# Some scaled copies of V on GpSimd, the gate in four pieces, new lengths and half sets in a planned attention kernel

## The chip, the cores and the metric

The kernel runs on one core of one Trainium2 chip. The metric is the time of the program on the device in microseconds (us), taken as the median of its runs. A core has five engines with one instruction queue each: TensorE (PE, matrix products), VectorE (DVE), ScalarE (ACT, here mostly exponentials), GpSimd (POOL) and SyncE (SP, which starts transfers). Each engine works through its own queue in order; semaphores tie the queues together.

## The reference

The input `x` has 2048 rows of 512 elements. Two blocks work on it and a gate mixes them:

```python
qkv = (x @ wqkv)...                      # 32 heads of 16
# block A
p = softmax(einsum("bhqd,bhkd->bhqk", q, k) * 16 ** -0.5)
a = einsum("bhqk,bhkd->bhqd", p, v) @ woA
# block B: linear attention, phi(t) = where(t > 0, t + 1, exp(t)) + 1e-6
num = phi(q) @ (phi(k)^T v);  den = phi(q) . sum(phi(k));  b = (num / den) @ woB
g = sigmoid((x * gate_w).sum(-1, keepdims=True))
return g * a + (1 - g) * b
```

Block A is nearly all of the work: 32 heads x 2048 x 2048 exponentials.

## The kernel before

**Rounds and units.** Block A runs in 32 rounds. A round is 4 heads against 512 queries; it is cut into 64 units, each of 128 keys of one head by 512 queries, so there are 2048 units in all. A unit takes one score product on PE ("QK": `ps<-Qpad,KT`, 512 columns), an exponential, and a product with V on PE.

**Two ways to the exponential.** Most units go to ACT (line 2063): one ACTIVATE takes the scores of two or three units out of PSUM, 1024 or 1536 columns wide, and writes `PT`. Other units are "claimed" for DVE (line 1565): DVE writes an integer into `DP` whose bits, read as a float, approximate the exponential. Such a unit is needed in three copies with shifted integers. Four claimed units make one tile of `DP`; the two shifted copies of a tile are made by one addition each, on POOL (line 1609) or on DVE (line 1606). Each of the three copies is multiplied by V times a weight of its own, so V is kept with the weights 1, 203/256 and 161/256. The two scaled copies of V exist only for the last six of the 16 key blocks (`KB2 = 10`), and claims come only from there. They are made in `step_V` (lines 895 to 927), by DVE (line 925): 288 or 576 columns each, 16 instructions in the whole kernel.

**Sets.** PE multiplies four units at once, one in each quarter of its columns: four matmuls of 32 output rows and 512 columns, called a set here (`pv_cols`, from line 1339). A set with `DP` is `ps<-DP,Vaug`, one with `PT` is `ps<-PT,Vaug`. In the last round, after 44 of the 64 units, the products are done the other way round, as matmuls of 52 columns (`ps<-Vaug,DP`, `ps<-Vaug,PT`).

**The ring.** The scores of a group of units (one ACTIVATE) lie in one of two slots of three PSUM banks (banks 0 to 2 and 3 to 5). PE may write the scores of group g+2 when ACT has read group g. Between two groups of score products PE does other work, called a gap here: sets, pieces of the projections, of block B and of the output, and fills (products with a tile of zeros, `ps<-warm`, which keep PE active).

**The planner.** The order of every queue is written out by a planner that runs when the kernel is built. It keeps a clock for each engine, adds a fixed length for each piece (`SET_T` for a set, `MM512` for a matmul of 512 columns, `QK_T` for the scores, `SWITCH_T` for a change of PE's tiling), and in the loop at lines 2089 to 2107 fills the gap after each group: sets when more than `PV_LAG` products wait, then a piece of another step (`misc_step`), then sets again, then fills. How many sets go into a gap is `room`: the time left before the next scores are late for ACT (`t_late`, with a reserve of `MARGIN`), divided by `SET_T`, plus `ROOM`, rounded down, at most `MOST`. Further constants bound claims (`CLAIM_LOAD`, `STARVE`), the lending of score banks (`LEND`), and the fills (`FILL_AHEAD`).

**DVE and POOL.** DVE's work waits in `items` and is picked by `pump`; an item with a second form may go to POOL (`pool_go`), unless DVE has work of its own that should go first (`YIELD`, `YIELD_SOON`).

**The gate.** `step_gate` (from line 937) multiplies `x` by `gate_w`: 64 matmuls of one column, in 16 pieces of four (`GATE_N = 1`), each piece in a gap of its own or beside sets.

**The end.** After the last exponential PE finishes the products of the last round, DVE normalises it (lines 1322, 1323), PE transposes it, adds the last block's output product, and four tiles of 128 rows are scaled and stored by ACT and DVE (lines 2159 and 2165).

Of the kernel before, what the change touches and what calls it, by code (L numbers as in the profile page):

```python
# [17 lines left out]
STATS = {}  # L18
# [165 lines left out]


LAT = 0.11
SET_T = 0.218
MM512 = 0.216
QK_T = 0.324

PVW = 26
WIDE_MAC = 0.4
PV_T = 0.1012
PV_MAC = 0.087
SWITCH_T = 0.095
SELF_T = 0.08
ROWS_SEEN = 0.0
ACT_END = 0.25
# [14 lines left out]
def bass_gated_mix__mha_block__linear_attn_block__prompt_kernel(  # L213
# [33 lines left out]
    with ExitStack() as es:  # L247
# [192 lines left out]
        port_ev = [None]  # L440
        boost = [None]
        ADD_W = 0.4
        YIELD = 1.2
        YIELD_SOON = 0.5
        POOL_TT = 1.3
        POOL_V = 0.9
        POOL_ADD = 1.97
        OT_POOL = 1
        V2_POOL = 0

        def conflicts(op_, reads, writes):
            r2, w2 = op_[1], op_[2]
# [231 lines left out]
        def f_mm(o, l, r, start=True, stop=True, sg=False):  # L684
            return lambda: nc.tensor.matmul(o, lhsT=l, rhs=r, start=start, stop=stop, skip_group_check=sg)  # L685
# [5 lines left out]
        def f_tr(o, i):  # L691
# [12 lines left out]
           dur=1.6)  # L704
# [225 lines left out]

        gate_done = []

        GATE_N = 1
        GATE_AT = 3.5
        GATE_MAC = 0.45

        def step_gate(**kw):
            rd = xt_all + [r_gw]
# [397 lines left out]
        done_j = {}  # L1336
        PV_UNITS = 2

        def pv_cols(now, r, force, want, most, least):

            urgent = sum(1 for e in pv_pending if e[3] in r_PT) > PT_URGENT
            mine = [e for e in pv_pending if e[0] == r]
            by_j = [collections.deque() for _ in range(4)]

            def ready(e):
                return not e[3].pw and e[3].tw + LAT <= now + 0.03 and v_ready(r, e[1])

# [10 lines left out]
            while len(sets) < most:  # L1358
# [12 lines left out]
            fns, rds = [], []  # L1371
            for s in sets:
                STATS["sets"] = STATS.get("sets", 0) + 1
                STATS["in_sets"] = STATS.get("in_sets", 0) + len(s)
                for e in s:
                    if not v_ready(r, e[1]):
                        ensure(lambda: v_ready(r, e[1]))
                    half = rounds[r][2]
                    kb, j = e[1] // 4, e[1] % 4
                    (p_ap, z), = e[2]  # L1380
                    v0 = v_of(t8 % 2, kb, 2 * j + half, z)
                    w = bass.AP(tensor=v0.tensor, offset=v0.offset, ap=[list(v0.ap[0]), [1, 32]])
                    fns.append(f_mm(acc[32 * j:32 * j + 32, :], w, p_ap, start=j not in started, stop=False, sg=True))
# [5 lines left out]
                    acc_n[0] += e[4]  # L1389
                    done_j[(r, j)] = done_j.get((r, j), 0) + e[4]  # L1390
                    pv_pending.remove(e)
            pe_macro(fns, reads=rds, writes=[r_acc], dur=SET_T * len(sets), mac=0.2 * len(sets), mode="cols")
            fresh[0] = False
            if acc_n[0] == NU:
                assert r < NR - 1
                round_end(r)
                acc_round[0] += 1
                acc_n[0] = 0
                fresh[0] = True
            elif r == NR - 1 and acc_n[0] >= PART:  # L1400
                assert len(started) == 4
                part[0] = 1
                fresh[0] = True
                push(0, [(lambda: nc.vector.tensor_copy(epool[:, 0, :], acc), [r_acc], [r_e[0]], d_psum(512), None),
                         (lambda: nc.vector.tensor_tensor(epool[:, 1, :], acc, epool[:, 0, :], ALU.subtract), [r_acc, r_e[0]], [r_e[1]],
                          d_psum(512), None)])
            return True
# [18 lines left out]
        def pv_step(now, force=False, want=None, most=3, least=4):  # L1426

            r = acc_round[0]
            if r >= NR:
# [12 lines left out]
            if fresh[0]:  # L1442
                started.clear()
            if r < NR - 1 or part[0] == 0:
                return pv_cols(now, r, force, want, most, least)
            if add_part(False):
                return True
            most = PV_UNITS * most
            sel = []
            if want is not None:  # L1450
# [401 lines left out]
        A_FIRST = 200  # L1852
        LATE_END = 0
# [126 lines left out]
        while True:  # L1980
# [112 lines left out]
            while PE.t < t_lim - 0.05:  # L2093
                pump(PE.t)
                behind = sum(1 for e in pv_pending if e[3] in r_PT) > (PV_LAG if act_round[0] < NR - 1 else LAG_END)
                enter = SWITCH_T if pe_mode[0] == "full" else 0.0
                room = min(MOST, int((t_late - PE.t - enter) / SET_T + ROOM))
                if behind and room > 0 and pv_step(PE.t, most=room, least=3):
                    continue
                if g > last_stage and misc_step(PE.t, t_late):  # L2100
                    continue
                if not behind and room > 0 and pv_step(PE.t, most=room):
                    continue
                if PE.t + FILL_T < t_lim and mac_until(max(t_lim, PE.t + FILL_AHEAD)) < (MAC_END if acc_n[0] >= END_FROM else MAC_LOW) and fill(PE.t):
                    continue
                PE.t += 0.05
# [248 lines left out]
```

## Time and profile before

| | |
|---|---|
| runs | 675.3, 675.98, 675.98 us, median 675.98 |
| the profiled execution | 675.2 us, of which the span from first to last instruction is 673.4 us |
| TensorE clock granted | 1.000 |
| ACT busy | 660.0 us (98%), 715 instructions |
| PE busy | 655.0 us (97%) |
| DVE busy | 576.0 us (86%) |
| POOL busy | 550.8 us (82%) |

"Busy" is the union of the instructions' records on an engine, and a matmul's record includes its way through the array, so records overlap. In the tables of groups a row gives the line, the engine, the operation, output and input with their shapes, the count, then busy time and mean duration in ns, then the idle time just before, with what ended it. In the timeline a row gives the start, the length, and a number of merged instructions.

### The profile page before, as it was taken

What the parts mean: (1) busy time and instruction counts of PE and PEld (TensorE: products, weight loads), DVE (VectorE), ACT (ScalarE), POOL (GpSimd) and SP (SyncE); (2) the same over time, 40 slices, a digit from 0 to 9 for tenths busy, and PEclk for the clock granted to TensorE, in tenths of its full rate; (3) what the DMA queues carried; (4) which work ended last, traced back from release to release, by engine and by line L of the source; (5) the groups of instructions that cost most, each with busy time, mean ns of one, the idle gap of its engine ahead of it and who ended that gap; (6) DMA issues with size and microseconds to landing.
All of it is one profiled execution on the core that took longest, in us unless ns stands there. A gap on an engine that the chain in (4) does not pass through costs nothing.

```text
span 673.4 us, 19207 instructions
## 1 busy us (share of the span) xinstructions
PE 655.0 (97%) x8078; PEld 200.1 (30%) x8080; DVE 576.0 (86%) x968; ACT 660.0 (98%) x715; POOL 550.8 (82%) x311
## 2 busy tenths in 40 slices
PE   8999999999999999999999999999999999999997
PEld 4322223333223232333222323323322222222223
DVE  4589889889887886888988998999889998989894
ACT  6999999999999999999999999999999999999995
POOL 5098889887889997788986999778788888898883
PEclk9999999999999999999999999999999999999999
DMA  9900101001010021101001010010211401010011
GB/s 221 252 3 12 24 2 31 6 11 27 1 35 2 18 50 35 32 2 29 7 10 35 10 41 11 16 29 13 46 26 24 52 25 42 10 44 24 20 41 44
DMA packets 44816, 22.96 MB, mean 34 GB/s; under 512 B 33976, under 2 KB 40568, under 8 KB 44728
## 3 DMA queue, kind: packets, MB, share of 16 engines
q1 hardware_dynamic: 42712, 20.12, 13.5%
q10 hardware_dynamic: 2016, 1.57, 0.9%
q8 instruction: 66, 1.08, 0.7%
q14 instruction: 22, 0.18, 0.1%
HBM read 8.00 MB, written 2.10 MB: 15 GB/s over the span
## 4 chain that ended last, share of the span: by engine, by line
ACT 95%; PE 4%; DMA 1%; DVE 1%; issue 0%; ACTq 0%
ACT PT L2063 92%; PE ps L685 3%; ACT epool L970 2%; DMA PT<-in_A_x_dram 1%; DVE DP L2165 0%; DVE xT L1909 0%; PE ps L692 0%; DVE KT L859 0%; DVE DP L2170 0%; DVE flag L2175 0%; ACT eg L954 0%; ACTq L2278 0%
## 5 line engine op out<-in xcount | busy, mean ns | idle before, releaser
L2063 ACT ACTIVATE PT<-ps 128x1024 bf16<-128x1024 f32 (+1 forms) x675 | 648.1, 1155 | 0.7 <-PE ps L685 0.5
L1609 POOL TENSOR_TENSOR DP<-DP,step 128x1024 int32<-128x1024 int32 x278 | 527.0, 1925 | 99.1 <-DVE DP L1565 27.6
L1565 DVE TENSOR_SCALAR DP<-ps 128x512 int16<-128x512 f32 x654 | 433.0, 685 | 69.1 <-PE ps L685 62.9
L685 PE MATMUL ps<-Qpad,KT 32*128 32x512 bf16 x2048 | 264.6, 384 | 10.0 <-ACT PT L2063 4.7
L685 PE MATMUL ps<-DP,Vaug 128*32 128x512 f16 x1949 | 206.8, 384 | 1.6 <-DVE oraw L1306 0.7
L685 PE MATMUL ps<-PT,Vaug 128*32 128x512 bf16 x1384 | 174.3, 384 | 0.6 <-DVE Vaug L914 0.5
L685 PEld LDWEIGHTS ps<-Qpad,KT 32*128 32x128 bf16 x2048 | 66.6, 91 | 269.9 <-ACT PT L2063 242.9
L685 PEld LDWEIGHTS ps<-DP,Vaug 128*32 128x32 bf16 x1949 | 49.7, 94 | 66.2 <-issue 41.1
L685 PEld LDWEIGHTS ps<-PT,Vaug 128*32 128x32 bf16 x1384 | 42.1, 95 | 46.7 <-issue 36.7
L685 PE MATMUL ps<-warm 128*32 128x512 bf16 (+1 forms) x272 | 46.7, 387 | 1.1 <-POOL step L735 1.1
L1606 DVE TENSOR_SCALAR DP<-DP 128x2048 int16<-128x2048 int16 (+1 forms) x50 | 33.4, 696 | 0.0
L685 PE MATMUL ps<-xT,wA 128*32 128x512 bf16 x432 | 32.6, 384 | 0.0
L1294 POOL TENSOR_TENSOR OT<-oraw,rbc 128x512 bf16<-128x512 f32 x12 | 15.6, 1302 | 11.3 <-DVE DP L1606 5.4
L970 ACT ACTIVATE epool<-ps 128x512 bf16<-128x512 f32 x32 | 23.4, 731 | 0.0
L1306 DVE COPY oraw<-ps 128x512 f32<-128x512 f32 x31 | 21.2, 682 | 0.7 <-PE ps L685 0.6
L685 PE MATMUL ps<-xT,wB 128*32 128x512 bf16 x256 | 19.7, 384 | 0.0
L685 PE MATMUL ps<-wB,xT 128*32 128x512 bf16 x256 | 19.3, 384 | 0.0
L685 PE MATMUL ps<-woA,OT 128*32 128x512 bf16 (+1 forms) x226 | 19.1, 384 | 0.0
L975 DVE SCALAR_TENSOR_TENSOR phi<-ps,epool 128x512 bf16<-128x512 f32 x24 | 16.3, 681 | 0.0
L685 PEld LDWEIGHTS ps<-warm 128*32 128x32 bf16 (+1 forms) x272 | 11.6, 98 | 13.8 <-issue 12.1
L859 DVE CAST KT<-ps 128x512 bf16<-128x512 f32 (+1 forms) x16 | 10.7, 667 | 5.2 <-PE ps L685 5.2
L685 PE MATMUL ps<-wA,xT 128*128 128x128 bf16 x192 | 14.9, 220 | 0.0
(106 smaller groups left out, 244.4 us busy)
## 6 DMA issues: line engine op xcount, KB each, us to landing
rbc<-oraw SPq DMA_DIRECT2D x16, 256.0 KB
OT<-in_A_x_dram SPq DMA_DIRECT2D x4, 512.0 KB, 7.1
Qpad<-Qs SPq DMA_DIRECT2D x124, 16.0 KB, 1.8
oraw<-oraw SPq DMA_DIRECT2D x60, 32.0 KB, 1.9
wA<-in_A_wqkv_dram SPq DMA_DIRECT2D x1, 1536.0 KB, 7.7
wB<-in_B_wqkv_dram SPq DMA_DIRECT2D x1, 1536.0 KB, 8.6
out_dram<-outt SPq DMA_DIRECT2D x12, 128.0 KB, 1.7
phi<-in_A_x_dram ACTq DMA_DIRECT2D x3, 256.0 KB, 6.1
```

The source lines that it names most:

```text
L685: return lambda: nc.tensor.matmul(o, lhsT=l, rhs=r, start=start, stop=stop, skip_group_check=sg)
L859: push(1, [(lambda: nc.vector.tensor_copy(KT[:, par, c0:c1], src), [r_bank[b]], [r_KT[par][t]], d_psum(n), None)])
L970: op(AC, lambda: nc.scalar.activation(epool[:, s, :], bank_ap(b), ACT.Exp), reads=[r_bank[b]], writes=[r_e[s]], dur=0.6, issue=0.48)
L975: (lambda: nc.vector.scalar_tensor_tensor(out=dst, in0=bank_ap(b), scalar=0.0, in1=epool[:, s, :], op0=ALU.max, op1=ALU.add), [r_bank[b], ...
L1294: push(1, [(lambda: (nc.gpsimd if on_pool else nc.vector).tensor_tensor(OT[:, t8, 512 * qc:512 * (qc + 1)], oraw[:, 0, :], rbc[:], ALU.mul ...
L1306: push(0, [(lambda: nc.vector.tensor_copy(oraw[:, half, :], acc), [r_acc], [r_oraw[half]], d_psum(512), evicted)])
L1565: push(0 if in_group else 1, [(lambda: nc.vector.tensor_scalar(DP[:, i, 512 * k:512 * (k + 1)].bitcast(I16), bank_ap(b), FRAC - Y_BIAS4, Y ...
L1606: ops = (lambda z=z, i2=i2, y=y, n=n: nc.vector.tensor_single_scalar(DP[:, i2, 0:n].bitcast(I16), y, STEPS[z], ALU.add), mine_, out_, d_sb ...
L1609: ops = (ops[0], mine_ + [r_step], out_, ops[3], None, POOL_ADD, lambda z=z, i2=i2, y=DP[:, i, 0:n].bitcast(I32), n=n: nc.gpsimd.tensor_te ...
L2063: op(AC, lambda p0=p0, b0=b0, n=n: nc.scalar.activation(PT[:, 512 * p0:512 * p0 + n], ps[:, 512 * b0:512 * b0 + n], ACT.Exp, scale=LN2 / F ...
```

## The change

GpSimd makes the scaled copies of V for all but the early steps (`V2_POOL = 1`). The gate's matmuls go in four pieces of 16. The planner's lengths are changed (`SET_T`, `MM512`, `SWITCH_T`, `GATE_MAC`), and so are constants of its choices. A set may be split into two halves of 256 columns, which may stand in different gaps: `pv_cols` puts the second half into `split` and issues it at the next opportunity, before any other set.

```diff
-SET_T = 0.218
-MM512 = 0.216
+SET_T = 0.223
+MM512 = 0.222
-SWITCH_T = 0.095
+SWITCH_T = 0.104
-        YIELD = 1.2
-        YIELD_SOON = 0.5
+        YIELD = 1.8
+        YIELD_SOON = 0.3
-        V2_POOL = 0
+        V2_POOL = 1
-        GATE_N = 1
+        GATE_N = 4
-        GATE_MAC = 0.45
+        GATE_MAC = 0.42
+        split = []
+        HALF_T = 0.12
+        ROOM_H = 0.4
-        def pv_cols(now, r, force, want, most, least):
+        def pv_cols(now, r, force, want, most, least, half=False):
+            if split:
+                s, fns, rds = split.pop()
+                pe_macro(fns, reads=rds, writes=[r_bank[acc_bank[0]]], dur=HALF_T, mac=0.1, mode="cols")
+                count(r, s)
+                return ended(r)
+            if half and most == 0 and len(started) < 4:
+                return False
...
+                    if most == 0:
+                        two.append([f_mm(acc[32 * j:32 * j + 32, c:c + 256], w, p_ap[:, c:c + 256], start=False, stop=False, sg=True)
+                                    for c in (0, 256)])
+            if most == 0:
+                pe_macro([a for a, _ in two], reads=rds, writes=[r_acc], dur=HALF_T, mac=0.1, mode="cols")
+                split.append((sets[0], [b for _, b in two], rds))
...
-        MOST = 4
+        MOST = 5
-        ROOM = 0.6
-        CLAIM_LOAD = 3.2
+        ROOM = 0.4
+        CLAIM_LOAD = 3.5
-        STARVE = 5
+        STARVE = 6
-        FILL_AHEAD = 0.9
+        FILL_AHEAD = 0.7
-        LEND = 140
-        RES_FROM = 60
-        MARGIN = 0.19
-        PV_LAG = 14
-        LATE = 12
+        LEND = 900
+        RES_FROM = 59
+        MARGIN = 0.17
+        PV_LAG = 13
+        LATE = 8
...
                 room = min(MOST, int((t_late - PE.t - enter) / SET_T + ROOM))
-                if behind and room > 0 and pv_step(PE.t, most=room, least=3):
+                half = room <= 0 and t_late - PE.t - enter > HALF_T * (1 - ROOM_H)
+                room = max(0, room)
+                if half and split and pv_step(PE.t, most=0, half=True):
+                    continue
+                if behind and (room > 0 or half) and pv_step(PE.t, most=room, least=3, half=half):
                     continue
...
-                if not behind and room > 0 and pv_step(PE.t, most=room):
+                if (room > 0 or half) and pv_step(PE.t, most=room, least=3 if room > 0 else 4, half=half):
                     continue
```

Because the planner decides from these numbers, the order of every queue is a new one from the first few microseconds on. Counted in the instruction listings of both kernels:

| instructions | before | after |
|---|---|---|
| ACT, exponentials of 1024 columns (two units) | 629 | 629 |
| ACT, exponentials of 1536 columns (three units) | 45 | 47 |
| DVE, claimed units | 654 | 648 |
| DVE, shifted copies of 2048 / 1024 columns | 48 / 2 | 53 / 0 |
| DVE, scaled copies of V | 16 | 4 |
| POOL, shifted copies | 278 | 271 |
| POOL, scaled copies of V, 288 / 576 columns | 0 / 0 | 6 / 6 |
| PE, matmuls of sets, 512 columns | 3333 | 2889 |
| PE, matmuls of half sets, 256 columns | 0 | 850 |
| PE, fills | 272 | 203 |
| PE, last round's matmuls of 52 columns | 92 | 120 |

More of the change, by code (lines that the diff above doesn't have):

```diff
@@ L1357, in pv_cols @@
             sets = []
-            while len(sets) < most:
+            while len(sets) < max(most, half):
                 s = [q[0] for q in by_j if q]
@@ L1370, in pv_cols @@
             t8 = rounds[r][0]
-            fns, rds = [], []
+            fns, rds, two = [], [], []
             for s in sets:
@@ L1388, in pv_cols, with count, ended @@
                             rds.append(res)
[L1389 to L1392 removed]
+                    if most == 0:
[4 more added lines that the diff above has]
+                split.append((sets[0], [b for _, b in two], rds))
+                STATS["halves"] = STATS.get("halves", 0) + 1
+                return True
+            pe_macro(fns, reads=rds, writes=[r_acc], dur=SET_T * len(sets), mac=0.2 * len(sets), mode="cols")
+            for s in sets:
+                count(r, s)
+            return ended(r)
+        def count(r, s):
+            for e in s:
+                acc_n[0] += e[4]
+                done_j[(r, e[1] % 4)] = done_j.get((r, e[1] % 4), 0) + e[4]
+                pv_pending.remove(e)
+        def ended(r):
+            acc, r_acc = acc_of(acc_bank[0]), r_bank[acc_bank[0]]
             fresh[0] = False
@@ L1424, in add_part, with pv_step @@
             return True
-        def pv_step(now, force=False, want=None, most=3, least=4):
+        def pv_step(now, force=False, want=None, most=3, least=4, half=False):
             r = acc_round[0]
@@ L1444, in pv_step @@
             if r < NR - 1 or part[0] == 0:
-                return pv_cols(now, r, force, want, most, least)
+                return pv_cols(now, r, force, want, most, least, half)
             if add_part(False):
                 return True
+            if most == 0:
+                return False
             most = PV_UNITS * most
```

## The prediction

> **What bounds the kernel now.** I read the busy times and the chain of work first, then the busy time by stages.
>
> ```profile
> PE 655.0 (97%) x8078; PEld 200.1 (30%) x8080; DVE 576.0 (86%) x968; ACT 660.0 (98%) x715; POOL 550.8 (82%) x311
> ...
> ACT 95%; PE 4%; DMA 1%; DVE 1%; issue 0%; ACTq 0%
> ```
>
> ```profile
> 200.00:300.00 100.00, 99.15 (x1275) 31.07 (x1272) 82.21 (x135) 100.00 (x107) 87.12 (x48) 1.00 0.11 24
> ...
> 500.00:600.00 100.00, 98.94 (x1238) 27.87 (x1234) 91.60 (x149) 100.00 (x107) 87.97 (x49) 1.00 0.17 31
> ```
>
> The stage rows hold the length, then busy time of PE, its loads, DVE, ACT and POOL, then PE's clock. ACT is the bound: its record is closed, 100.00 of 100, even where PE looks just as full. The question is whether this closed record hides room. The groups by shape, and ACT's queue in order of time, answer it.
>
> ```profile
> L2063 ACT ACTIVATE PT<-ps 128x1024 bf16<-128x1024 f32 x629 | 590.9, 1130 | 0.0
> L2063 ACT ACTIVATE PT<-ps 128x1536 bf16<-128x1536 f32 x45 | 65.1, 1517 | 0.6 <-PE ps L685 0.5
> L970 ACT ACTIVATE epool<-ps 128x512 bf16<-128x512 f32 x32 | 23.4, 731 | 0.0
> ```
>
> ```profile
> 9.18 22.06 ACT L2063 ACTIVATE PT<-ps 128x1536 bf16<-128x1536 f32 x18 [0.52 <-PE ps L685]
> ...
> 162.42 0.63 ACT L970 ACTIVATE epool<-ps 128x512 bf16<-128x512 f32 x1
> 162.90 6.99 ACT L2063 ACTIVATE PT<-ps 128x1536 bf16<-128x1536 f32 x7
> 169.65 0.73 ACT L970 ACTIVATE epool<-ps 128x512 bf16<-128x512 f32 x1
> 170.13 4.83 ACT L2063 ACTIVATE PT<-ps 128x1024 bf16<-128x1024 f32 x5
> ...
> 504.67 160.34 ACT L2063 ACTIVATE PT<-ps 128x1024 bf16<-128x1024 f32 x167
> ```
>
> Ends tell more than starts here, because ACT's instructions overlap. The small exponential ends at 169.65 + 0.73 = 170.38, the five two-unit ones at 170.13 + 4.83 = 174.96: 4.58 us for five, **0.916 us each**. The seven before them (one of three units, six of two) end at 169.89, and the small one ahead of them at 163.05: 6.84 us, less 6 x 0.916 leaves **1.34 us** for three units. A small one takes 170.38 - 169.89 = 0.49. So the exponentials cost at least 629 x 0.916 + 45 x 1.34 + 32 x 0.49 = 576.2 + 60.3 + 15.7 = 652.2, with the rest of the digits about 653 us. They run from 9.18 to 504.67 + 160.34 = 665.01, which is 655.8. **About 2.6 us is all that PE ever made ACT lose**; the reader should see that a better order of PE's work can win no more than that, whatever PE's busy share says. The rest of the span is 9.18 us ahead and 8.4 behind.
>
> Where do the 2.6 us come from? PE's queue in a dense stretch:
>
> ```profile
> 279.28 0.39 PE L685 MATMUL ps<-Qpad,KT 32*128 32x512 bf16 x3
> 279.61 0.61 PE L685 MATMUL ps<-phi,OT 128*32 128x512 bf16 x8
> 280.15 0.39 PE L685 MATMUL ps<-Qpad,KT 32*128 32x512 bf16 x3
> 280.48 0.82 PE L685 MATMUL ps<-PT,Vaug 128*32 128x512 bf16 x9
> 280.92 0.38 PE L685 MATMUL ps<-DP,Vaug 128*32 128x512 f16 x1
> 280.92 0.38 PE L685 MATMUL ps<-PT,Vaug 128*32 128x512 bf16 x2
> 281.24 0.39 PE L685 MATMUL ps<-Qpad,KT 32*128 32x512 bf16 x3
> ```
>
> From scores to scores, two sets (or eight projection matmuls) take 0.87 us, three take 1.09. So a set costs 0.22, and scores with their switches about 0.43. Against ACT's 0.916 two sets leave 0.05 spare and three are 0.17 over; a run of gaps with 3, 2, 2 just breaks even, and more than that starves ACT.
>
> **The change, part by part.** The counts are from the two instruction listings.
>
> *Exponentials on ACT.* Six units fewer are claimed (654 to 648), and they come back as two more ACTIVATEs of three units, with the 629 of two unchanged: 2 x 1.34 = **+2.7 us** on the bounding engine. Nothing hides it.
> The Trainium skill (ScalarE: Activation LUTs, section "What ACT_TABLE_LOAD costs") gives 0.833 ns per element plus 186 ns for an ACTIVATE with immediate scale and bias, so as an estimate from it two instructions of 1536 cost between 2.6 us (overlapped) and 2.9 us (alone). The 2.7 of the rows lies between these; by the page the sum would move by 0.2 us at most.
>
> *Half sets and new lengths.* 3333 set matmuls become 2889 whole ones and 850 halves. The only matmuls of 32 x 256 in the trace are in the start:
>
> ```profile
> 9.07 0.62 PE L685 MATMUL ps<-xT,outt 128*32 128x256 bf16 x16
> ```
>
> Four quads in 0.62, as long as two quads of 512 columns above: a half costs 0.11 (0.155 if the whole length counts). I take 0.11, so that splitting is nearly free; at 0.155 the 212 halves add 10 us to PE, no more than what the dropped fills give back (272 to 203, 69 x about 0.17 us from the row below). What it brings: gaps of work worth three sets fall from 132 to 19, while those worth 2.5 rise from 14 to 115. I added PE's prices down both listings, sixteen groups at a time, against ACT's prices for the same groups. Before, 10 of 40 stretches are over, by 2.2 us together, which is nearly the whole 2.6 us. After, one of 41 is over, by 0.1. So nearly all that PE's volume cost is won: I take **-1.8 us**. What stays is about 0.3 us in the start, whose groups hardly change, and 0.5 for waits on other engines. Bounds: -2.6 if all goes, and above zero if the new order brings waits of its own (rival C).
>
> ```profile
> L685 PE MATMUL ps<-warm 128*32 128x512 bf16 (+1 forms) x272 | 46.7, 387 | 1.1 <-POOL step L735 1.1
> ```
>
> *Gate in four pieces.* The pieces of before take 0.17 us between their neighbours:
>
> ```profile
> 135.00 0.24 PE L685 MATMUL ps<-gw,xT 128*128 128x1 bf16 x4
> 135.17 0.39 PE L685 MATMUL ps<-Qpad,KT 32*128 32x512 bf16 x3
> ```
>
> Sixteen in a row are at most 4 x 0.17 = 0.7 us; with scores 1.1, once 0.2 over ACT's 0.916. Three of the four pieces stand between ordinary gaps that leave spare; cost between -0.1 and +0.5, I take 0. It frees PE some 2 us that it doesn't need.
>
> *V copies to GpSimd.*
>
> ```profile
> L925 DVE TENSOR_SCALAR Vaug<-Vaug 128x576 bf16<-128x576 bf16 x8 | 2.4, 302 | 0.0
> L925 DVE TENSOR_SCALAR Vaug<-Vaug 128x288 bf16<-128x288 bf16 x8 | 1.7, 218 | 0.0
> L1609 POOL TENSOR_TENSOR DP<-DP,step 128x1024 int32<-128x1024 int32 x278 | 527.0, 1925 | 99.1 <-DVE DP L1565 27.6 <-DVE epool L973 21.7 <-DVE DP L1606 14.9
> L1294 POOL TENSOR_TENSOR OT<-oraw,rbc 128x512 bf16<-128x512 f32 x12 | 15.6, 1302 | 11.3 <-DVE DP L1606 5.4 <-DMA rbc<-oraw 2.5 <-DVE Vaug L925 2.0
> ```
>
> DVE is rid of 12 copies, 6 x (0.30 + 0.22) = 3.1 us. On POOL the price is not in the trace: DVE's durations below, the 2.5 ns per column of line 1294 above, so 3 to 13 us for the twelve. I take 10. Seven shifted copies fewer free 7 x 1.9 = 13.5, so POOL is not fuller. Its queue gains a wait: a copy waits for DVE's V, and the shifted copies behind it wait too, and PE's `DP` sets for those. POOL has 99 us of idle time ahead of line 1609, and the scaled V is needed rounds later. On the path: 0.
>
> *The end.* Here the order changes for the worse.
>
> ```profile
> 663.27 0.38 PE L685 MATMUL ps<-Qpad,KT 32*128 32x512 bf16 x1
> 663.76 0.96 PE L685 MATMUL ps<-Vaug,DP 128*128 128x52 bf16 x32
> 664.57 0.61 PE L685 MATMUL ps<-identb,epool 128*128 128x128 bf16 x8
> 665.01 0.27 PE L685 MATMUL ps<-Vaug,DP 128*128 128x52 bf16 x4
> 665.11 1.16 PE L685 MATMUL ps<-Vaug,PT 128*128 128x52 bf16 x40
> 666.12 0.56 PE L685 MATMUL ps<-Vaug,DP 128*128 128x52 bf16 x16
> 666.74 0.81 PE L685 MATMUL ps<-woB,OBT 128*128 128x512 bf16 x3
> ```
>
> Before, 92 narrow matmuls finish the last round; 40 cost 666.12 - 665.11 = 1.01, or 0.025 each. From the last scores to the products' end it is about 3.4 us, and ACT's last exponential ends at 665.01, 1.7 before that end. After, behind the last scores stand two matmuls of 512 columns, 24 narrow ones, the eight of `epool`, then 96 narrow ones: 0.43 + 0.43 + 0.6 + 0.44 + 2.4 = 4.3 us. The last scores may come when the last ACTIVATE of three units has read its banks; then two units (0.92) and one (0.49) follow, so ACT ends 1.4 us after them and the products 2.9 after ACT, against 1.7. That is +1.2, and one more output matmul stands before the transposes, some 0.1: **+1.3 us**. Bounds: +0.5 (if PE's earlier work is done sooner) to +2.2 (if these products also wait for POOL's last copy, as two of their waits allow).
>
> *Sum.* 675.2 (profiled) + 2.7 - 1.8 + 1.3 = 677.4. The profiled execution is the lowest of the four known times, whose mean is 675.6, and the metric is a median, so I add 0.5: **677.9 us**, 0.3% over the median of 675.98.
>
> **Rivals.**
> A. *Not slower:* ACT's lost time goes to nothing and the end gains only its lower bound: 675.98 + 2.7 - 2.6 + 0.5 = 676.6, within 0.2% of 675.98. It decides if PE's last products stay level with ACT's end. For it: 16-group stretches with almost no excess. Against: the end's order. Faster than 674.6 needs ACT to do its added work in less time than the rows show.
> B. *GpSimd late:* if copies hold up POOL's queue, PE, in order, stands at a `DP` set while the scores behind it wait. Each costs what exceeds ACT's reserve.
>
> ```profile
> PE ps L685 <- POOL DP L1609: 0.3, 2, 0.2
> ```
>
> The longest of these waits is 0.2 us, and only 0.3 us in all are put down to POOL's copies, which speaks against the rival. I price 12 copies with a wait half as long again, 0.3 us: 677.9 + 3.6 = 681.5. The Trainium skill (GPSIMD Engine Reference, section "Engine selection") speaks against the move: it wants elementwise work on VectorE and only calls one-input work roughly line-rate on GpSimd. No run here shows that yet; by it the copies are at the lower half of my bounds.
> C. *Planned too tight:* `MARGIN` is smaller, `MOST` larger and fewer fills stand between, so that errors of the plan's lengths add up to new stops; twice the old loss gives 677.9 + 2.6 + 1.8 = 682.3. Or PE's clock falls with fewer fills; it is 1.00 in every stage now. Against it: the new set length of 0.223 is above the measured 0.22, so PE will be ahead of its plan.
> D. *The change doesn't do what it says:* 4 of 16 copies stay on DVE; the listings show the other parts, so this has no separate time.
>
> **How the numbers follow.** Forecast (677.3 to 679.5) 0.55; A 0.25, of which hardly any below 674.6; B 0.10; C 0.10. I split A as 0.22 within and 0.03 faster. A measurement of this kernel can tell about 0.2%, 1.35 us, from no change: slower (over 677.3) 0.75, same 0.22, faster 0.03. The range leaves out the lowest part of A and most of B and C: 676.0 to 681.0.
>
> **What would show it.** Line 2094 with 677 instructions, 47 of them of 1536 columns, and 0.9 us more from the first exponential to the end of the last (2.7 less 1.8); PE's gaps of 0.98 us in place of 1.09; last products ending 2.9 us after the last exponential. Wrong if ACT's row shows idle time put down to PE or POOL, if the clock of a stage is below 1.00, or if the end is not longer.

## The result, and the profile after

Six runs of each kernel gave 678.11 us after (677.79 to 678.25) against 675.64 before (675.12 to 675.99): a ratio of 1.0034, with a 95% interval of 1.0024 to 1.0043. The kernel is **slower by 0.34%**, where 677.9 us was forecast. The profiled execution took 677.98 us, with a span of 676.2.

The page of the kernel after: busy times and chain by engine.

```profile
PE 655.8 (97%) x8445; PEld 207.6 (31%) x8445; DVE 574.7 (85%) x953; ACT 660.8 (98%) x717; POOL 543.5 (80%) x316
...
ACT 86%; PE 10%; DVE 2%; DMA 1%; POOL 0%; issue 0%; DVEq 0%; ACTq 0%
```

ACT still has most of the chain that ended last; PE has 10% of it where it had 4%. How much ACT stood still is said by its own rows, by shape and in order of time.

```profile
L2094 ACT ACTIVATE PT<-ps 128x1024 bf16<-128x1024 f32 x629 | 594.5, 1240 | 0.2 <-PE ps L685 0.2
L2094 ACT ACTIVATE PT<-ps 128x1536 bf16<-128x1536 f32 x47 | 69.8, 1615 | 0.7 <-PE ps L685 0.5
L970 ACT ACTIVATE epool<-ps 128x512 bf16<-128x512 f32 x32 | 26.5, 827 | 0.0
```

```profile
253.58 76.13 ACT L2094 ACTIVATE PT<-ps 128x1024 bf16<-128x1024 f32 x81 [0.23 <-PE ps L685]
...
349.69 0.80 ACT L970 ACTIVATE epool<-ps 128x512 bf16<-128x512 f32 x1
350.17 14.99 ACT L2094 ACTIVATE PT<-ps 128x1024 bf16<-128x1024 f32 x16
```

Two things are to be seen. The mean *duration* of a two-unit ACTIVATE rose from 1130 to 1240 ns, though its price did not: the small exponential ends at 349.69 + 0.80 = 350.49, the sixteen behind it at 350.17 + 14.99 = 365.16, which is 14.67 / 16 = 0.917 each, as before. The records overlap, and in this kernel they overlap more: longer records go here with less lost time, so the mean duration is no price. And behind the start ACT's timeline has one stop ahead of an exponential, at 253.58.

To account for a whole run I set the end of each exponential against the end before it plus its price. The prices, from ends as in the prediction, are 0.9165 (two units), 1.3435 (three) and 0.49 (one unit, or a small one). The sum of prices is called service here, what exceeds it lost time. (In 18 of 20 stretches of 33.67 us the kernel after loses less than 0.01 us by these prices, so they fit. The columns add up to 0.1 less than the span, because the record of the first exponential is that much longer than its price.)

| profiled execution, us | first exponential starts | service | lost | from the last exponential's end to the span's end | span |
|---|---|---|---|---|---|
| before | 9.18 | 653.18 | 2.54 | 8.4 | 673.4 |
| after | 9.19 | 655.87 | 0.84 | 10.2 | 676.2 |
| difference | 0.0 | +2.69 | -1.70 | +1.8 | +2.8 |

Of the lost 0.84, 0.34 lies in the start, as before, and 0.40 around 253.6. The rows there, DVE, PE and POOL of the kernel after in order of time:

```profile
249.19 3.20 DVE L1637 TENSOR_SCALAR DP<-DP 128x2048 int16<-128x2048 int16 x2
...
249.95 1.89 POOL L1640 TENSOR_TENSOR DP<-DP,step 128x1024 int32<-128x1024 int32 x1 [0.66 <-DVE DP L1637]
...
252.31 0.68 DVE L859 CAST KT<-ps 128x512 bf16<-128x512 f32 x1
...
253.14 0.40 PE L685 MATMUL ps<-Qpad,KT 32*128 32x512 bf16 x4 [0.70 <-DVE KT L859]
...
253.46 0.62 PE L685 MATMUL ps<-PT,Vaug 128*32 128x512 bf16 x8
...
253.91 0.28 PE L685 MATMUL ps<-DP,Vaug 128*32 128x256 f16 x4
...
254.12 0.39 PE L685 MATMUL ps<-Qpad,KT 32*128 32x512 bf16 x3
```

Of the two shifted copies on DVE, which share the first row, the second started 0.01 us behind POOL's addition and took 2.44 us; the cast of K behind it was late too, and PE waited 0.70 us for K. The last four rows also hold a gap of two and a half sets: scores at 253.14, the next at 254.12, so 0.98 us, as forecast. (It is a typical one: the 50 gaps of this kernel that hold two whole sets and a half one have a median of 0.98.)

The end of the kernel after, on PE, on POOL and on DVE:

```profile
664.81 0.39 PE L685 MATMUL ps<-Qpad,KT 32*128 32x512 bf16 x1
665.13 0.61 PE L685 MATMUL ps<-woA,OT 128*128 128x512 bf16 x2
665.57 0.77 PE L685 MATMUL ps<-Vaug,DP 128*128 128x52 bf16 x24
666.18 0.61 PE L685 MATMUL ps<-identb,epool 128*128 128x128 bf16 x8
666.62 1.53 PE L685 MATMUL ps<-Vaug,DP 128*128 128x52 bf16 x48
668.00 1.36 PE L685 MATMUL ps<-Vaug,PT 128*128 128x52 bf16 x48
669.20 0.38 PE L685 MATMUL ps<-woA,OT 128*128 128x512 bf16 x1
```

```profile
665.04 2.28 POOL L1640 TENSOR_TENSOR DP<-DP,step 128x1024 int32<-128x1024 int32 x1 [0.73 <-DVE OT L1285]
```

```profile
669.40 0.26 DVE L1322 RECIPROCAL rraw<-ps 128x16 f32<-128x16 f32 x1 [3.83 <-PE ps L685]
```

The same row of the kernel before:

```profile
666.72 0.26 DVE L1322 RECIPROCAL rraw<-ps 128x16 f32<-128x16 f32 x1 [2.44 <-PE ps L685]
```

The last ACTIVATE ends at 666.00, and DVE starts on the finished products at 669.40: 3.4 us later. Before, DVE started on them at 666.72, for an end at 665.01: 1.7. From the last scores to the products' end it is now 4.55 us (664.81 to 669.36), where 4.3 was forecast, and ACT ends 1.2 us after these scores, where 1.4 was forecast. The last 48 narrow matmuls with `PT` took 669.20 - 668.00 = 1.20, the 48 with `DP` ahead of them 1.38; POOL's last copy ended among these, at 667.32.

The copies of V on POOL:

```profile
L922 POOL TENSOR_SCALAR Vaug<-Vaug 128x576 bf16<-128x576 bf16 x6 | 4.0, 672 | 9.3 <-DVE DP L1637 6.3 <-DVE epool L973 2.8
L922 POOL TENSOR_SCALAR Vaug<-Vaug 128x288 bf16<-128x288 bf16 x6 | 2.6, 432 | 0.5
```

They cost 6.6 us of POOL's time (10 were assumed), and no wait of PE in this profile is put down to them.

### The profile page after: what moved, and what is told of

Its sections match the earlier page's. It is cut to its first block, busy times and chain, and to the rows that moved or that the text cites. A ratio compares the mean times of both kernels' runs of the same rounds, so it can differ in the third digit from the quotient of the medians.

```text
span 676.2 us, 19908 instructions
## 1 busy us (share of the span) xinstructions
PE 655.8 (97%) x8445; PEld 207.6 (31%) x8445; DVE 574.7 (85%) x953; ACT 660.8 (98%) x717; POOL 543.5 (80%) x316
## 4 chain that ended last, share of the span: by engine, by line
ACT 86%; PE 10%; DVE 2%; DMA 1%; POOL 0%; issue 0%; DVEq 0%; ACTq 0%
ACT PT L2094 84%; PE ps L685 10%; ACT epool L970 2%; DVE DP L1596 1%; DMA PT<-in_A_x_dram 1%; DVE DP L1637 0%; POOL DP L1640 0%; DVE DP L2200 0%; DVE xT L1940 0%; DVE KT L859 0%; DVE phi L1136 0%; DVE epool L1433 0%; PE ps L692 0%; DVE Vaug L914 0%; DVE dev L1253 0%
## 5 line engine op out<-in xcount | busy, mean ns | idle before, releaser
L1640 POOL TENSOR_TENSOR DP<-DP,step 128x1024 int32<-128x1024 int32 x271 | 513.0, 1922 | 102.8 <-DVE DP L1596 29.8
L685 PE MATMUL ps<-DP,Vaug 128*32 128x512 f16 (+1 forms) x2269 | 219.0, 352 | 1.9 <-DVE phi L975 0.3
L685 PE MATMUL ps<-PT,Vaug 128*32 128x512 bf16 (+1 forms) x1470 | 182.6, 372 | 0.5 <-DVE Vaug L914 0.5
L685 PEld LDWEIGHTS ps<-DP,Vaug 128*32 128x32 bf16 x2269 | 60.0, 95 | 75.6 <-issue 48.0
L685 PEld LDWEIGHTS ps<-PT,Vaug 128*32 128x32 bf16 x1470 | 48.1, 95 | 43.1 <-issue 34.6
L1637 DVE TENSOR_SCALAR DP<-DP 128x2048 int16<-128x2048 int16 x53 | 38.0, 740 | 0.1
L685 PE MATMUL ps<-warm 128*32 128x512 bf16 (+1 forms) x203 | 33.7, 391 | 1.1 <-POOL step L735 1.1
L922 POOL TENSOR_SCALAR Vaug<-Vaug 128x288 bf16<-128x288 bf16 (+1 forms) x12 | 6.6, 552 | 9.8 <-DVE DP L1637 6.3
```

Source lines behind the costliest of these rows:

```text
L922: ops.append((lambda z=z: nc.gpsimd.tensor_scalar(v_scaled(par, z, kb, n), src2, WEIGHTS[z], 1.0, ALU.mult, ALU.mult), [r_V[par][v]], [r_V ...
L1637: ops = (lambda z=z, i2=i2, y=y, n=n: nc.vector.tensor_single_scalar(DP[:, i2, 0:n].bitcast(I16), y, STEPS[z], ALU.add), mine_, out_, d_sb ...
L1640: ops = (ops[0], mine_ + [r_step], out_, ops[3], None, POOL_ADD, lambda z=z, i2=i2, y=DP[:, i, 0:n].bitcast(I32), n=n: nc.gpsimd.tensor_te ...
```

## The experiments

Theory: ACT's counts set the service, which goes into the time in full; the lost time and the end come on top; a change to the planner's lengths acts through the claims that the planner can make, whatever it does on PE. Rivals: the shorter pieces themselves or POOL's copies cost time, or ACT's price isn't what binds. All ratios are against the kernel before.

### Six exponentials of three units more, nothing else

```diff
 op(AC, lambda: nc.scalar.activation(PT[...], ps[...], ACT.Exp, ...))
+if len(us) == 3 and g >= 60 and len(twice) < 6 and (not twice or g >= twice[-1] + 12):
+    op(AC, ...)   # the same again; the planner's clock is left as it was
```

> The kernel before, its order kept, with six of its ACTIVATEs of three units issued a second time (same input, same output). Theory (ACT's own work sets the time, 1.34 us for each such instruction): 6 x 1.34 = 8.1 us more, less at most 1 us of ACT's old lost time, so 682.6 to 683.8 us against 675.6. Rival (PE, 97% busy, is as much the bound, so that ACT's work hides beside it): below 678.5 us.

Measured: 685.5 us (684.7 to 691.04), ratio 1.0161 (1.0134 to 1.0188). In the profiled execution the service is 661.24, which is 8.06 = 6 x 1.3435 more, and the lost time rose by 2.1: 0.14 at each of the six, which read and write the same tiles as the instruction before it, and 1.2 at one place where PE's clock fell:

```profile
124.00:126.00 2.00, 0.83 (x13) 0.19 (x7) 1.32 (x3) 1.97 (x3) 2.00 (x2) 1.00 0.01 4
126.00:128.00 2.00, 1.54 (x27) 0.74 (x31) 1.10 (x2) 2.00 (x3) 2.00 (x2) 0.68 0.04 4
128.00:130.00 2.00, 2.00 (x23) 0.28 (x15) 0.75 (x2) 1.18 (x2) 1.48 (x1) 0.50 0.04 8
```

The stage rows of that kernel: PE (second number) stood idle for 1.2 of the 2 us from 124, and from some 126.7 to 130.1 the clock (the number behind POOL's) was half. What follows: ACT's price of a three-unit ACTIVATE goes into the time in full, so the first term of the prediction stands. The time passed the expected 682.6 to 683.8 by the 0.14 at each of the six and by what falls of the clock added: the two runs with a mean clock of 1.000 took 684.7 and 684.93, which is 9.1 and 9.3 more than before, against 8.06 + 6 x 0.14 = 8.9.

### The parts alone

Each of these is the kernel before with one part of the change.

The half sets (the code of `split`, with `HALF_T` and `ROOM_H`; all other constants of before):

> The kernel before with the half sets alone, all constants old. Theory (the time follows ACT's work in the new order, what PE's stretches exceed it by, and the end): 56 ACTIVATEs of three units and 616 of two are 2.4 us more than before, PE's stretches of sixteen are over by 2.8 us against 2.2, the end is 0.7 us shorter: 677.9 us, range 677 to 679. Rival (halves alone bring less lost time and a gain): 675 us or less.

The gate in four pieces:

```diff
-GATE_N = 1
+GATE_N = 4
-GATE_MAC = 0.45
+GATE_MAC = 0.42
```

> The kernel before with the gate in four pieces alone. Theory (as for the half sets alone): 61 ACTIVATEs of three units, 609 of two and one of one are 3.2 us more than before, stretches over by 2.0 us against 2.2, the end 1.5 us longer, since 108 narrow matmuls stand in it: 680.1 us, range 679 to 681.2. Rival (a larger piece only moves PE's work): 675.6 us within 0.7.

The three lengths:

```diff
-SET_T = 0.218
-MM512 = 0.216
+SET_T = 0.223
+MM512 = 0.222
-SWITCH_T = 0.095
+SWITCH_T = 0.104
```

> The kernel before with the three new lengths alone (set, 512 columns, switch). Theory (ACT's work in the new order, excess of PE's stretches, end): 63 ACTIVATEs of three units and 611 of two are 7.2 us more, stretches over by 3.4 us against 2.2, the end 0.4 shorter: 683.5 us, range 682.5 to 685. Rival (longer planned lengths keep PE ahead of its plan and so win): below 675.

The copies of V on GpSimd (`V2_POOL = 1`):

> The kernel before with GpSimd making the scaled copies of V alone. Theory (as for the lengths alone): 61 ACTIVATEs of three units and 614 of two are 7.3 us more, stretches over by 4.1 us against 2.2, the end the same: 684.7 us, range 683.5 to 686. Rival (the copies on GpSimd cost time by themselves, through waits for POOL's queue): over 686, with PE's waits put down to POOL; a third view, that 3 us less work on DVE is a gain: below 675.

Measured, with the account of the profiled execution (of the half sets that one took 678.02, the least of its five runs, so its account is short of the median by 1.2 us):

| kernel | median, us | ratio (95%) | two / three units | first | service | lost | end |
|---|---|---|---|---|---|---|---|
| half sets | 679.24 | 1.005 (1.0037 to 1.0063) | 616 / 56 | 9.08 | 655.56 | 4.00 | 7.5 |
| gate | 679.59 | 1.0058 (1.0045 to 1.0071) | 609 / 61 | 9.17 | 656.35 | 2.20 | 10.0 |
| lengths | 681.59 | 1.009 (1.0074 to 1.0105) | 611 / 63 | 9.16 | 660.38 | 1.95 | 7.9 |
| V on GpSimd | 685.18 | 1.015 (1.0134 to 1.0165) | 614 / 61 | 9.28 | 660.44 | 4.43 | 8.7 |

The counts are in the group rows; those of the last kernel, with PE's longest wait for DVE (in all, times, longest):

```profile
L2063 ACT ACTIVATE PT<-ps 128x1024 bf16<-128x1024 f32 x614 | 579.8, 1138 | 1.0 <-PE ps L685 0.6
L2063 ACT ACTIVATE PT<-ps 128x1536 bf16<-128x1536 f32 x61 | 88.0, 1538 | 0.7 <-PE ps L685 0.5
```

```profile
PE ps L685 <- DVE DP L1565: 2.0, 5, 0.7
```

Each part alone is slower than before, and each than the four together, though for the half sets the interval still overlaps that of the kernel after. The larger share is not lost time: with V on GpSimd, PE has no wait for a copy of V. What each part does is give the planner other numbers, and it then claims fewer units for DVE (648, 646, 637 and 637, in the order of the table, against 654 before), so that ACT has 2.4 to 7.3 us more service. The half sets alone also lose 1.5 us more than before, and PE's waits for POOL's shifted copies there come to 1.9 us in six waits, where they were 0.3. For the gate and for V the expected ranges held, and the half sets came 0.2 us above theirs. For the lengths the time came 0.9 us below the range: the lost time was 1.95 (1.26 of it at one place), not 3.4 or more. That longer planned sets keep PE ahead of its plan would explain this, and is not shown. So "what half sets cost" has no answer of its own in this kernel; an answer needs the order held.

### Whole sets in the order of after

Where the kernel after issues the first half of a split set, this one issues both halves in a row, and nothing where the second half stood (the lines for that are left out below); all else keeps its place. The matmuls stay 256 columns wide, so what is undone is the spreading over two gaps.

```diff
-pe_macro([a for a, _ in two], reads=rds, writes=[r_acc], dur=HALF_T, ...)
+pe_macro([a for a, _ in two] + [b for _, b in two], reads=rds, writes=[r_acc], dur=HALF_T, ...)
...
```

> The changed kernel with its order kept, but each split set runs whole in the place of its first half, so that gaps of 2.5 sets become 3 and 2 again. Theory 1 (ACT's lost time fell because each stretch of sixteen groups now holds less of PE's work than ACT needs, not because the pieces are small): no stretch is over, so 678.1 us within 0.4, and ACT's lost time stays at 0.8 us within 0.4. Theory 2 (the halves themselves won it, since a gap of three sets is 0.17 us over ACT's 0.916): 0.5 to 2 us of lost time come back, 678.8 to 680 us.

Measured: 679.46 us (678.06 to 680.95), ratio 1.0046 (1.0033 to 1.0059). In the profiled execution ACT lost 3.59 us, 2.87 of them in one stretch:

```profile
366.00:368.00 2.00, 1.24 (x11) 0.29 (x9) 2.00 (x5) 2.00 (x3) 1.20 (x1) 1.00 0.33 66
368.00:370.00 2.00, 1.57 (x18) 0.34 (x15) 1.98 (x4) 2.00 (x3) 2.00 (x2) 0.79 0.01 4
...
374.00:376.00 2.00, 2.00 (x24) 0.56 (x20) 0.81 (x3) 1.08 (x2) 2.00 (x2) 0.50 0.00 0
376.00:378.00 2.00, 2.00 (x38) 0.64 (x30) 2.00 (x4) 2.00 (x3) 1.63 (x1) 1.00 0.00 0
```

PE was busy for 1.24 of the 2 us from 366; then its clock was 0.50 from 369.2 to 376.0, and ACT (fifth number) fell to 1.08 of 2. The kernel after stops at the same place, and there the clock stays:

```profile
366.00:368.00 2.00, 1.35 (x19) 0.33 (x11) 2.00 (x6) 2.00 (x3) 1.04 (x1) 1.00 0.35 73
368.00:370.00 2.00, 1.69 (x20) 0.45 (x20) 1.97 (x5) 2.00 (x3) 2.00 (x2) 1.00 0.03 5
```

Outside that stretch the lost time is 0.7, where after has 0.84, of which 0.40 is the wait at 253.6 that this execution does not have. The median lies in the range of theory 2, but two of the five runs had a clock below 1.000; of the three at 1.000, two took 678.06 and 678.1, as theory 1 says, and the third 679.46, for which there is no trace. So, where the clock holds, the trace speaks for theory 1: the lost time was won by the order's load per stretch of groups, not by spreading the sets over two gaps. Whether whole sets make a fall of the clock likelier is not shown; in the six runs of the kernel after no mean clock was below 0.999.

### No fills

The fills after the start are left out, with every other instruction in its place.

> The changed kernel, its order and plan kept, without any of its fills after the start. Theory (fills are spare work and serve only PE's clock; 272 to 203 of them are still enough): the clock falls in places and ACT loses time there, some 3 us for each fall as in the kernel with whole sets, so 685 us or more, granted clock below 0.99. Rival (fills have no use, fewer of them are free): 678.1 us within 0.5, clock 1.00.

Measured: 683.16 us (681.16 to 685.89), ratio 1.011 (1.0082 to 1.0137), less than the 685 that were expected at least; mean clocks of 0.983 to 0.992. Lost time 6.64, nearly all where the clock fell: for 3.4 us at 35.8 and at 100.6, and for 13.7 us from 363.4:

```profile
363.00:366.00 3.00, 2.90 (x21) 0.58 (x21) 2.25 (x4) 2.79 (x4) 2.99 (x2) 0.57 0.32 67
366.00:369.00 3.00, 3.00 (x25) 0.85 (x22) 0.83 (x2) 2.25 (x3) 0.00 (x0) 0.50 0.03 5
```

So the second half of rival C, a fall of the clock with fewer fills, is real. The kernel after runs at a clock of 1.00 without the 69 fills that the change drops; of the 203 that stay, the 190 behind the start could not all go. The three falls cost 1.0, 0.9 and 4.2 us of lost time, 0.25 to 0.31 us for each us at half a clock.

### A shorter end

Of the 120 narrow matmuls behind the last scores, 54 are left out, so part of the last round's products is missing from the output.

```diff
-fns += pv_fns(e[0], e[1], p_ap, z, fresh[0] and n == 0, w)
+part_fns = pv_fns(e[0], e[1], p_ap, z, fresh[0] and n == 0, w)
+fns += part_fns if e[3] in r_PT else part_fns[:1]
```

> The changed kernel, its order kept, leaving out three of four narrow matmuls of each product of a DP copy in the last round (54 of 120 narrow matmuls). Theory (the end is PE's chain of narrow products, which runs past ACT's last exponential): 54 x 0.025 = 1.4 us less, 676.7 us within 0.4, products ending 2.0 us after ACT in place of 3.4. Rival (the end waits for POOL's and DVE's last copies, PE is only beside them): at most 0.4 us less.

Measured: 677.59 us (677.37 to 678.11), ratio 1.0031 (1.0018 to 1.0043): 0.5 less by the medians, 0.4 by the distances from before, where PE does 54 x 0.025 = 1.4 less. In the profiled execution the end is 9.8 us in place of 10.2. PE and POOL at its end:

```profile
664.89 2.27 POOL L1641 TENSOR_TENSOR DP<-DP,step 128x1024 int32<-128x1024 int32 x1 [0.73 <-DVE OT L1285]
...
667.22 0.32 PE L685 MATMUL ps<-Vaug,DP 128*128 128x52 bf16 x6 [0.90 <-POOL DP L1641]
...
667.39 1.37 PE L685 MATMUL ps<-Vaug,PT 128*128 128x52 bf16 x48
```

With less to do, PE stands for 0.90 us at the products that need POOL's last copy (664.89 + 2.27 = 667.16). So the end was held by two chains of almost equal length, PE's products and POOL's last copy: 1.35 less the wait of 0.90 is the 0.45 by which the end got shorter. The expectation, which gave all of it to the products, missed by 0.9 us; its rival, at most 0.4, is nearer.

### Other constants for the same four parts

If the counts decide, then constants (nine are changed here) for which the planner finds an order with less service should win, with all four parts in place.

```diff
-SET_T = 0.223
+SET_T = 0.217
-POOL_V = 0.9
+POOL_V = 0.7
-PT_URGENT = 12
+PT_URGENT = 11
-HALF_T = 0.12
-ROOM_H = 0.4
+HALF_T = 0.112
+ROOM_H = 0.6
-ROOM = 0.4
+ROOM = 0.6
-STARVE = 6
+STARVE = 7
-MARGIN = 0.17
+MARGIN = 0.19
-LATE = 8
+LATE = 12
```

> The kernel after, with eight of the planner's constants set otherwise (SET_T 0.217, POOL_V 0.7, PT_URGENT 11, HALF_T 0.112, ROOM_H 0.6, ROOM 0.6, STARVE 7, MARGIN 0.19, LATE 12); all four parts of the change stay. In its order ScalarE makes 620 exponentials of two units and 50 of three, against 629, 47 and one of one unit after: one claim more of GpSimd. Theory 1 (the time is ScalarE's service from the counts plus little lost plus the end): service 651.2 by the prices of the traces (0.9165, 1.3435), 4.7 us less than after; lost time 1 to 2; the end, with 68 narrow matmuls behind the last scores instead of 120, about 1.5 to 2 us shorter. 671 to 674 us, faster than both kernels. Rival (the order with fewer exponentials was bought with rows of PE work at places where PE then is late, or the clock falls): lost time over 4 us, 675 us or more, no faster than before.

A second set (`SET_T` 0.217, `HALF_T` 0.112, `MARGIN` 0.19, `GATE_MAC` 0.4, `CLAIM_LOAD` 2.9, `LATE_CLAIM` 3, `FILL_AHEAD` 0.8):

> The kernel after with seven other constants (SET_T 0.217, HALF_T 0.112, MARGIN 0.19, GATE_MAC 0.4, CLAIM_LOAD 2.9, LATE_CLAIM 3, FILL_AHEAD 0.8); all four parts of the change stay. 626 exponentials of two units and 48 of three: by the prices of the traces a service of 654.0 us, 1.9 less than after; 60 narrow matmuls behind the last scores. Theory 1: 673.5 to 676 us, some 2 to 4 less than after. Rival (lost time or a fall of the clock takes it back): 677 us or more.

Measured: the first 675.4 us (674.3 to 676.41), ratio 0.9997 (0.9988 to 1.0006); the second 675.08 (674.83 to 675.76), ratio 0.9994 (0.9985 to 1.0003). Both are faster than after and neither differs from before beyond its interval. The second came as expected: service 653.97, lost 1.47. The first has the 651.16 us of service that its counts promised, but lost 4.56, so that its time lies in the rival's range: a sum of counts alone is not the time. More than a third of the loss is at one place. Its timeline there:

```profile
466.76 0.67 POOL L922 TENSOR_SCALAR Vaug<-Vaug 128x576 bf16<-128x576 bf16 x1 [0.89 <-DVE epool L973]
...
467.39 1.89 POOL L1640 TENSOR_TENSOR DP<-DP,step 128x1024 int32<-128x1024 int32 x1
...
469.06 0.68 DVE L891 TENSOR_SCALAR Qs<-ps 128x512 bf16<-128x512 f32 x1
...
469.37 0.67 POOL L922 TENSOR_SCALAR Vaug<-Vaug 128x576 bf16<-128x576 bf16 x1
...
470.09 0.28 PE L685 MATMUL ps<-PT,Vaug 128*32 128x256 bf16 x1 [1.74 <-POOL Vaug L922]
...
470.76 2.37 ACT L2094 ACTIVATE PT<-ps 128x1024 bf16<-128x1024 f32 x2 [1.66 <-PE ps L685]
```

This is the wait of rival B, in another order than the one forecast: a copy of V stands in POOL's queue behind a shifted copy of 1.89 us, PE in order behind it, and ACT loses 1.77 us.

### The late copy of V first

The kernel just shown, with POOL's last copy of V issued ahead of that shifted copy; and the kernel just shown once more beside it.

```diff
...
+if dur == POOL_V:
+    n_v[0] += 1
+    if n_v[0] == 12:
+        (w0, f0, i0, s0), (w1, f1, i1, s1) = E.ops[-2:]
+        E.ops[-2:] = [(w0 + w1, f1, i0, s0), ([], f0, i1, s1)]
+        ev.idx, po_last[0].idx = po_last[0].idx, ev.idx
...
```

> The kernel of consts_a with one thing moved: GpSimd's twelfth (last) scaled copy of V is issued ahead of the shifted copy that stood between it and the eleventh; no other queue's order changes. In consts_a TensorE waited 1.74 us for this copy (put down to line 922, at 470.09) and ScalarE's exponential there came 1.77 us late. Theory (that place in GpSimd's queue is what the wait was): the wait is gone, lost time 2.8 us instead of 4.56, and the time 1.2 to 1.8 us less than consts_a, 673.3 to 674.2 us, faster than before by 0.2 to 0.35%. Rival (the shifted copy that now comes 0.67 us later holds TensorE up at a set of its own, or the wait only moves to the next scores): 674.8 us or more, no different from consts_a.

> The kernel of consts_a once more, beside v_first on the same chip, so that the two can be compared under the same conditions. Both theories: 675.4 us within 0.5, and the wait for line 922 of 1.7 us again.

Measured: 674.93 us (674.0 to 676.9) against 676.08 for before beside it, **ratio 0.9986 (0.9977 to 0.9995)**: the one version whose interval lies below before as well as after, by 0.14% against before. It lies in the rival's range all the same (674.8 or more). The repeated kernel gave 676.4 (674.37 to 677.1), ratio 0.9999 (0.999 to 1.0008), half a us above the range expected of it, with the wait of 1.7 us again, and with something that its first profile had not:

```profile
466.00:470.00 4.00, 2.26 (x29) 0.71 (x28) 3.48 (x7) 3.03 (x4) 3.20 (x3) 1.00 0.00 0
470.00:472.00 2.00, 1.97 (x27) 0.79 (x31) 1.31 (x3) 1.31 (x2) 1.89 (x1) 0.77 0.19 37
472.00:474.00 2.00, 2.00 (x18) 0.62 (x10) 1.09 (x3) 1.36 (x2) 1.68 (x1) 0.50 0.18 41
474.00:476.00 2.00, 2.00 (x23) 0.45 (x21) 1.68 (x3) 1.46 (x2) 2.00 (x2) 0.88 0.11 30
```

The same stop of PE was followed here by half a clock for some 3.4 us (the missing parts of three rows: 0.46 + 1.0 + 0.24 = 1.7 us at a clock lower by half), and between 465 and 487 us ACT lost 1.5 us more. Six of its eleven runs had a mean clock of 0.996 or 0.997 and took 676.4 to 677.1; the five with 1.000 took 674.37 to 675.5. With the copy ahead, the wait is gone, and PE's waits between 465 and 486 us are these:

```profile
PE ps L695 <- DVE Qs L901: 0.8, 1, 0.8
PE ps L695 <- DVE DP L1606: 0.2, 1, 0.2
```

So the wait for the copy mostly moved to the next scores, which now wait for DVE's `Qs`; in the first kernel that stood just behind, at 469.06 + 0.68 = 469.74. The account by stretches says what the move is worth, since in all three executions the order is the same but for this pair:

| ACT's lost time, us | 0 to 200 | 200 to 300 | 300 to 465 | 465 to 487 | behind |
|---|---|---|---|---|---|
| the kernel of the other constants | 0.90 | 1.25 | 0.03 | 1.81 | 0.56 |
| the same once more | 0.89 | 0.28 | 0.03 | 3.35 | 0.57 |
| copy of V first | 0.89 | 0.80 | 0.03 | 1.52 | 0.57 |

At its place the move saves 0.3 us where the clock holds and 1.8 where it falls. The medians say the same: 674.93 lies 1.5 us below the repeated kernel, but 0.3 below that kernel's five runs at 1.000, whose middle is 675.19. So the rival was right about the wait, and most of the gain is that the clock no longer falls there. The stretch from 200 to 300 us shows how much two executions of one order differ by themselves.

## Why the prediction was right

Right in sign and size, and in the mechanism of its largest term, ACT's added work. The end was mis-sized, luck hid that in the total, and the credit that the prediction gave to the half sets is not borne out.

- **The bound.** ACT's exponentials, priced from ends, as the bound: shown. Six more of them cost 8.06 us of service, and they came out in the time (9.9 us between the medians, with what the waits and the clock added).
- **Exponentials, +2.7:** +2.69 of service by the finer prices. By the Trainium skill (ScalarE: Activation LUTs, section "What ACT_TABLE_LOAD costs"), as an estimate, one of 1536 columns takes 1.47 us alone, and the overlap of some 93 ns that the section gives for ACTIVATEs in a row makes it 1.37; the measured 1.34 is 0.03 below that.
- **Lost time, -1.8:** measured -1.70. The 0.8 us that were to stay are there, 0.34 in the start and most of the rest at one wait on another engine. By that wait one of the prediction's signs of being wrong shows in small: ACT's row has 0.2 us put down to PE, where it had 0.0. From the first exponential to the end of the last it is 1.0 us more, where 0.9 was forecast. The count of gaps by stretches of sixteen groups was a good predictor for this order. For the parts alone, with 0.34 added for the start, it gave 2.3 and 4.4 for the gate and for V (measured 2.20 and 4.43), but 3.1 for the half sets (4.00) and 3.7 for the lengths (1.95). The prediction put the gain down to the half sets; the run with whole sets, outside its fall of the clock, speaks for the order instead.
- **Half a set, 0.11:** the gap of two and a half sets took 0.98 us, as forecast; the bound of 0.155 did not come.
- **Gate, 0:** from scores to scores a piece takes 130.50 - 129.64 = 0.86 us, below the 1.1 allowed and below ACT's 0.916.

```profile
129.64 0.39 PE L685 MATMUL ps<-Qpad,KT 32*128 32x512 bf16 x3
129.96 0.55 PE L685 MATMUL ps<-gw,xT 128*128 128x1 bf16 x16
130.50 0.39 PE L685 MATMUL ps<-Qpad,KT 32*128 32x512 bf16 x3
```

- **V copies, 10 us on POOL and 0 on the path:** 6.6 us on POOL, 0 on the path. The duration was taken too high by half, and that did not matter. The Trainium skill's preference for VectorE (GPSIMD Engine Reference, section "Engine selection") is borne out by the durations, 672 ns on POOL against 302 on DVE for 576 columns, a factor of 2.2; it shows in no wait of this order. That one-input work is roughly line-rate on GpSimd, as the same section of the Trainium skill has it, does not mean DVE's pace here.
- **The end, +1.3:** mis-sized; it was +1.8. The products ended 3.4 us after ACT's end, not 2.9: they came 0.25 later after the last scores, and ACT ended 0.2 sooner. The prediction named POOL's last copy as a bound (+2.2) and did not use it; the shorter end shows that this copy and PE's products end almost together.
- **Basis, +0.5:** the profiled execution of after lies 0.13 below its median, where 0.5 was added. The 0.4 too much here hid the 0.5 too little at the end.

Of the rivals, A (all lost time gone, the end only 0.5 longer) did not come, since 0.84 us stay lost and the end is 1.8 longer. B and C did not come either: the longest wait of PE for POOL's `DP` is 0.2 us, and the clock is 1.00. D is out by the rows, twelve copies on POOL. Yet B and C both appear in neighbouring orders, in another form than priced. B was one wait of 1.74 us, not twelve of 0.3, and taking it away saved 0.3 us where the clock held. C's falls of the clock cost 0.9 to 4.2 us each.

What stays open: why the planner claims fewer units with the change than without. The runs show that each part lowers the claims by itself and that other constants raise them again; which decision of the planner is the first to differ was not followed. The change also sets twelve constants of the planner's choices (`YIELD` to `LATE`), which no run sets alone, so what the four parts owe to them, the better lost time above all, is open.

## What to carry to other kernels

Where one engine's record is closed, count its instructions and price them from their ends: here that priced the added work of ACT to 0.1 us, while mean durations moved without meaning a cost. An order that a planner writes from assumed lengths moves by several microseconds with them (651 to 660 us of service in the orders here), so a part is judged with the order held, not by switching it on. A wait that a profile puts down to one engine is worth only the distance to the next limit: a wait of 1.74 us gave back 0.3. The last microseconds want a look of their own, at every engine that feeds them, since two chains of equal length make either one look like the bound.

## What the runs showed of the hardware

- PE's clock halved after some short stops and not after others. It was 0.50 for about 3.4, 6.8 and 13.7 us; ahead of it PE had been busy for 0.83 of 2 us, or 1.24 of 2, while 1.35 of 2 at the same place of the kernel after brought no fall. No run here shows where the limit lies. The same kernel had a mean clock below 1.000 in six runs of eleven in one measurement, and its two profiled executions had the same wait of 1.7 us, one with the fall and one without.
- When a shifted copy on DVE and an operation of POOL overlap, the one that starts second is held up. In the kernel after 21 of POOL's additions started while a copy was running: the copies kept their 0.69 us, the additions took 2.27 in place of 1.89 (medians). Three copies started well inside an operation of POOL: each ended 0.55 us behind the end of that operation, and they took 0.80, 1.76 and 2.44 us. The copies' row gives shortest, middle and longest in ns:

```profile
L1637 DVE TENSOR_SCALAR DP<-DP x53: 677/685/2436, 47.6 to 664.9; 128x2048 int16<-128x2048 int16 x53
```

- The same kernel began its exponentials at 9.08 us in one profiled execution and at 9.99 in another, so the start alone moves a single run by 0.9 us.
